# One-hot rows by transposes instead of DMA at the start of an attention and snake-MLP kernel, and the preparation of batch 0 dealt out anew

## The chip, the cores and the metric

The kernel runs on one core of one Trainium2 chip. The metric is the device time of one execution in microseconds (us). A time here is the median of several executions. Executions of one kernel mostly agree within 0.3 to 0.5%, but a few lie 0.3 to 0.7% higher. One core only is in use, so no two dies can be compared.

PE is the tensor engine (PEld its weight loads), DVE the vector engine, ACT the scalar engine, POOL the engine that here casts to bf16 and issues most loads, SP the engine that issues most other DMAs.

## The reference, cut to what matters

```python
q_assign = argmax(q_n @ c_n)          # nearest of 16 centroids, per token; k likewise
mask = q_assign[..., :, None] == k_assign[..., None, :]
attn = softmax(where(mask, q @ k.T / 8, -1e9))     # 4 batches, 8 heads, 768 tokens, 64 wide
x = (attn @ v) as 3072 x 512
h = x @ w_in;  out = (h + sin(alpha*h)**2 / alpha) @ w_out     # 512 -> 2048 -> 512
```

## The kernel before

The mask is folded into the score matmul. Each q and k column has 64 rows of data and 16 more rows that hold the one-hot of its centroid, so that one matmul over 80 rows gives scores and mask together. A *pair* is two heads; a batch has four pairs, and a pair takes 12 *steps*. One step is a score matmul (one k tile of 128 against 768 q), an exponential on ACT, and PV matmuls.

A pair must be prepared before its steps begin. Four *transpose units* (`prep_T`) turn q and k of both heads, each through one PSUM bank, which DVE or ACT then empties. A *routing unit* multiplies by the centroids, DVE finds the maximum and makes the one-hot (`prep_hot`), and DMAs carry it from its 128-partition layout to rows 64 to 79 of `QK` (`prep_move`, eight DMAs of one pair). A plan says at which step each of these stands.

```python
    def head_move(m, h, engs):                      # rows of one head, four DMAs
        for g in range(4):
            hf, t = divmod(g, 2)
            engs[t].dma_start(out=QK[D:D+NHC, m % NQK, h, t]..., in_=s["ohT"][32*g:32*g+NHC, :, 0:QS])
    # ... (cut) the start:
    warmup(2)
    head_asn(0, 0, M0)                               # routing matmuls, pair 0, head 0
    prep_cast(0, 0)
    for i in range(4):
        prep_hot(0, i, QS)                           # DVE: transpose, max, one-hot, transpose back
    prep_T(0, 2, SA[0][:, 0:512], "act")
    prep_T(0, 3, M1, "act")
    head_move(0, 0, [nc.sync, nc.scalar])
    load_qk(2)
    # ... (cut)
    head_move(0, 1, [nc.sync, nc.sync])
    prep_T(1, 0, M2, "act")                          # pair 1, all four, ahead of the first score
    prep_T(1, 2, M1)
    prep_T(1, 1, M0, "act")
    prep_T(1, 3, OB)
    load_v(1)
    warmup(1)
    # ... (cut) the plan of batch 0: (pair, transpose units at, routing unit at, casts at)
        (1, (), 1, (0, 0)),
        (2, ((0, 4), (2, 5), (1, 6), (3, 7)), 8, (7, 8)),
        # ...
    for m, i in {3: 5, 4: 10, 5: 12, 6: 18, 7: 22}.items():   # loads of q and k at
        at(i, lambda m=m: load_qk(m, eng=nc.gpsimd))
    at(39, alpha)                                    # one PE transpose, three small DVE operations
```

A PE transpose that must wait for its bank holds up the score matmul written after it: in the changed kernel below, the second score comes at 12.66 us, behind a transpose that waited until 12.28.

The softmax here doesn't subtract the row's maximum and nothing guards it: scores larger than these inputs give would overflow.

Of the kernel before, what the change touches and what calls it, by code (L numbers as in the profile page):

```python
# [10 lines left out]
BF16 = mybir.dt.bfloat16  # L11
# [4 lines left out]
P = 128  # L16
# [6 lines left out]
def kernel(  # L23
# [11 lines left out]
    nc = tc.nc  # L35

    B, H, S, D = q.shape
    NHC = centroids.shape[1]
# [6 lines left out]
    HS = S // 2  # L45
    QS = S // 4
# [22 lines left out]
    OB = psum.tile([P, 512], F32, name="OB")  # L69
    M0 = psum.tile([P, 512], F32, name="M0")  # L70
    M1 = psum.tile([P, 512], F32, name="M1")
    M2 = psum.tile([P, 512], F32, name="M2")

    ident_f = const.tile([P, P], F32, name="ident_f")
    ident_b = const.tile([P, P], BF16, name="ident_b")
# [6 lines left out]
    NQK = 6  # L82
    KR = D + NHC
    QK = const.tile([96, NQK, 2, 2, S], BF16, name="QK")
# [6 lines left out]
    st = [dict() for _ in range(NP)]  # L91
# [10 lines left out]
    def bank():  # L102
        while True:
            i = turn[0] % 3
            turn[0] += 1
            if i not in held:
                return banks[i]


    def load_qk(m, parts=1, eng=None):  # L110
        b, hp = pair_of[m]
        s = st[m]
        for nm in ("q32", "k32"):
            s[nm] = ldp.tile([P, 2, NJ * D], F32, tag=nm, name=nm)
        for i in range(parts):
            n = 2 // parts
            for nm, src in (("q32", q), ("k32", k)):
                (eng or nc.sync).dma_start(
                    out=s[nm][:, n * i : n * i + n, :],
                    in_=src[b, 2 * hp + n * i : 2 * hp + n * i + n].rearrange(  # L120
                        "h (p j) d -> p h (j d)", j=NJ
                    ),
                )
# [11 lines left out]
    def prep_T(m, g, bk=None, eng="dve"):  # L135

        s = st[m]
        if "T32" not in s:
            s["T32"] = trp.tile([P, 4, HS], F32, tag="T32", name="T32")
        h, t = divmod(g, 2)  # L140
        src = s["q32" if t == 0 else "k32"]
        bk = bank() if bk is None else bk
        for jj in range(NJ2):
            nc.tensor.transpose(  # L144
                out=bk[:, P * jj : P * jj + P],
                in_=src[:, h, P * jj : P * jj + P],
                identity=ident_f,
            )
        if eng == "dve":
            nc.vector.tensor_scalar_mul(  # L150
                out=s["T32"][:, g, :], in0=bk[:, 0:HS], scalar1=1.0 / QDIV
            )
        else:
            nc.scalar.activation(
                out=s["T32"][:, g, :], in_=bk[:, 0:HS], func=ACTF.Copy, scale=1.0 / QDIV
            )
# [24 lines left out]
    def prep_cast(m, h, eng=None):  # L181
        s = st[m]
        for par in range(2):
            src = s["T32"][D * par : D * par + D, 2 * h : 2 * h + 2, :]
            if m < NPE:
                nc.gpsimd.tensor_copy(  # L186
                    out=QK[0:D, m % NQK, h, :, HS * par : HS * par + HS], in_=src
                )
                continue
            for t in range(2):  # L190
                nc.gpsimd.tensor_scalar(  # L191
                    out=QK[0:D, m % NQK, h, t].rearrange("c (n i a) -> c i n a", i=4, a=32)[
                        :, 2 * par : 2 * par + 2
                    ],
                    in0=src[:, t].rearrange("c (i n a) -> c i n a", i=2, a=32),
                    scalar1=1.0 / QDIV,
                    scalar2=1.0,
                    op0=ALU.mult,
                    op1=ALU.mult,
                )  # L200

    def prep_v(m):
        nc.gpsimd.tensor_copy(out=VX[m % NVX][:, :, :, 0:D], in_=st[m]["v32"])  # L203
# [18 lines left out]
    def head_asn(m, h, bk):  # L222

        s = st[m]
        hp = pair_of[m][1]
        for g in range(4):
            hf, t = divmod(g, 2)
            nc.tensor.matmul(
                out=bk[32 * g : 32 * g + 32, 0:QS],
                lhsT=cnB[:, 2 * hp + h, :],  # L230
                rhs=s["T32"][:, 2 * h + t, QS * hf : QS * hf + QS],
                start=True,
                stop=True,
            )
        s["asn"] = bk[:, 0:QS]
# [69 lines left out]
    def head_move(m, h, engs):  # L305
        s = st[m]
        for g in range(4):
            hf, t = divmod(g, 2)
            engs[t].dma_start(
                out=QK[D : D + NHC, m % NQK, h, t].rearrange("c (par n) -> c par n", par=2)[  # L310
                    :, :, QS * hf : QS * hf + QS
                ],
                in_=s["ohT"][32 * g : 32 * g + NHC, :, 0:QS],
            )


    def area(i):
        return SA[(i // ASTEPS + i) % 2]

# [40 lines left out]
    def x_T(m, bk=None):  # L360
        b, hp = pair_of[m]
        xs = st[m]["xs"]
        xt_ps = (bank() if bk is None else bk).bitcast(BF16)[:, 0:S]
        for j in range(NJ):
            nc.tensor.transpose(
                out=xt_ps.rearrange("c (i j a) -> c j i a", i=4, j=NJ)[:, j],
                in_=xs[:, j, :, :],
                identity=ident_b,
            )
        nc.vector.tensor_copy(out=xT[:, hp, :], in_=xt_ps)  # L370
        st[m].clear()
# [127 lines left out]
    def warmup(n):  # L499
        for _ in range(n):  # L500
            nc.tensor.matmul(
                out=SA[1][:, 512:1024],
                lhsT=warm[:, 0:P],
                rhs=warm[:, P:640],
                start=True,
                stop=True,
            )
# [5 lines left out]
        out=csq, in0=c_sb, scalar=1.0, in1=c_sb, op0=ALU.mult, op1=ALU.mult, accum_out=cnrm  # L513
# [7 lines left out]
        out=cn_dup, in0=c_sb.unsqueeze(1).to_broadcast([P, 2, D]), scalar1=crn[:, 0:1]  # L521
# [4 lines left out]
    for h0, h1 in ((0, 1), (1, H)):  # L526
        for par in range(2):
            rows = slice(D * par, D * par + D)
            nc.vector.tensor_copy(
                out=cnB[rows, h0:h1, NHC * par : NHC * par + NHC],  # L530
                in_=OB[rows, NHC * h0 : NHC * h1].rearrange("p (h c) -> p h c", c=NHC),
            )
    etab = const.tile([P, 1], F32, name="etab")
    nc.scalar.activation(out=etab, in_=crn, func=ACTF.Exp)
    warmup(2)
    head_asn(0, 0, M0)
    prep_cast(0, 0)
    for i in range(4):
        prep_hot(0, i, QS)
    prep_T(0, 2, SA[0][:, 0:512], "act")  # L540
    prep_T(0, 3, M1, "act")
    head_move(0, 0, [nc.sync, nc.scalar])
    load_qk(2)
    prep_cast(0, 1)
    prep_v(0)
    head_asn(0, 1, OB)
    for i in range(4):
        prep_hot(0, i, QS)
    head_move(0, 1, [nc.sync, nc.sync])
    prep_T(1, 0, M2, "act")  # L550
    prep_T(1, 2, M1)
    prep_T(1, 1, M0, "act")
    prep_T(1, 3, OB)
    load_v(1)
    warmup(1)
    alpha_col = const.tile([P, NF], F32, name="alpha_col")
    ralpha = const.tile([P, NF], F32, name="ralpha")

# [3 lines left out]
    def at(i, fn):  # L562
        plan.setdefault(i, []).append(fn)
# [21 lines left out]
    def prep_new(m, k0):  # L585
# [4 lines left out]
        at(k0 + 17, lambda: prep_cast(m, 1))  # L590
        hot_steps(m, k0 + 8)

    for m, make, asn, cast in (
        (1, (), 1, (0, 0)),
        (2, ((0, 4), (2, 5), (1, 6), (3, 7)), 8, (7, 8)),
        (3, ((0, 12), (1, 14), (2, 16), (3, 17)), 20, (14, 18)),
        (4, ((0, 19), (1, 23), (2, 24), (3, 26)), 32, (24, 28)),
        (5, ((0, 28), (1, 30), (2, 31), (3, 34)), 38, (31, 35)),
        (6, ((0, 35), (1, 36), (2, 37), (3, 40)), None, (37, 41)),
    ):  # L600
        pair_steps(m, make, asn, cast)
    for g, i in enumerate((41, 42, 43)):
        at(i, lambda g=g: prep_T(NHP + 3, g))
    for h in range(2):
        at(ASTEPS + 4 + 2 * h, lambda h=h: prep_cast(NHP + 3, h))
    hot_steps(NHP + 3, ASTEPS + 7)
    for m, i in {3: 5, 4: 10, 5: 12, 6: 18, 7: 22}.items():
        at(i, lambda m=m: load_qk(m, eng=nc.gpsimd))
    late = []
    pacer = const.tile([1, 1], BF16, name="pacer")  # L610
    for b in range(1, B):
        for n in range(NHP):
            m = NHP * b + 3 + n
            if NPE <= m < NP:
                prep_new(m, ASTEPS * b + STEPS * n)
                if m < 3 * NHP:
                    late.append(m)
                else:
                    at(2 * ASTEPS - 1, lambda m=m: load_qk(m, eng=nc.gpsimd))
# [4 lines left out]
    for m in range(NP):  # L624
        if m % NHP != NHP - 1:
            if m < NHP:
                at((18, 29, 44)[m], lambda m=m: x_T(m))
            elif m % NHP == 2:
                at(STEPS * (m + 1) + 4, lambda m=m: x_T(m))
            else:  # L630
                at(STEPS * (m + 1) + 5, lambda m=m: x_D(m))
# [8 lines left out]
        nc.vector.tensor_scalar_add(out=ralpha, in0=alpha_col, scalar1=1e-9)  # L640
        nc.vector.reciprocal(out=ralpha, in_=ralpha)

    at(39, alpha)
    def load_w_in(n):
        nc.gpsimd.dma_start(
            out=w_in_bf[:, :, 512 * n : 512 * n + 512],
# [26 lines left out]
    for b in range(B):  # L673
        base = ASTEPS * b
        fill = Fill(b - 1) if b else None
        for r in range(ASTEPS):
            i = base + r
# [105 lines left out]
```

## Time and profile before

| | before |
|---|---|
| time, median | 313.26 us (312.94 to 313.51, 4 executions) |
| granted clock of the profiled execution | 1.000 |
| first score matmul | 11.39 us |
| first and last exponential of batch 0 start | 11.91 and 52.94 us |

So a wait on PE in the early stage is time lost, unless something else was to be waited for anyway.

The timeline of PE around the first score (start, length, engine, line, operation; in brackets the idle time before it and what ended it):

```profile
9.44 0.52 PE L144 MATMUL M<-ident_f,k 128*128 128x128 f32 x3 [0.21 <-DMA k<-in_k_dram]
9.79 0.49 PE L144 MATMUL OB<-ident_f,k 128*128 128x128 f32 x3
10.12 0.38 PE L501 MATMUL S<-gT 128*128 128x512 bf16 x1
11.39 0.38 PE L326 MATMUL S<-QK 80*128 80x512 bf16 x1 [0.89 <-DMA QK<-ohT]
11.61 0.27 PE L327 MATMUL S<-QK 80*128 80x256 bf16 x1
11.71 0.38 PE L326 MATMUL S<-QK 80*128 80x512 bf16 x1
```

The first score waits 0.89 us for the DMA of the one-hot rows, and the second follows 0.3 us later. That wait is what the change goes after. The largest waits of PE from 9 to 60 us (total, number, longest; that of L425, at 59.74 us, is already past batch 0):

```profile
PE S L326 <- DMA QK<-ohT: 1.2, 2, 0.9
PE S L425 <- DVE gT L450: 0.6, 1, 0.6
PE M L144 <- DVE T L150: 0.6, 1, 0.6
```

From the start times of the exponentials in the trace, a step takes 0.69 to 0.74 us with no unit in it, 0.85 to 0.87 us with a transpose unit, and 1.2 to 1.4 us around a routing unit.

### The profile page before, as it was taken

How to read it: one execution, taken by the hardware profiler on the slowest of the kernel's cores; microseconds unless marked ns; L12 is line 12 of the kernel's file. 1: busy time of each engine (PE TensorE's matmuls, PEld its weight loads, DVE VectorE, ACT ScalarE, POOL GpSimd, SP SyncE). 2: the span in 40 equal slices, each digit the busy share in tenths (PEclk: the TensorE clock that was granted, in tenths of full speed). 3: DMA queues.
4: the chain of work that ended last, by engine and by line, in shares of the span. 5: the costliest groups of instructions: out<-in, count | busy, mean ns of one | idle time of the engine just before them, and what ended most of it. 6: DMA issues, size and time to landing. Idle time of an engine off the chain costs nothing.

```text
span 312.8 us, 7228 instructions
## 1 busy us (share of the span) xinstructions
PE 302.7 (97%) x2750; PEld 179.9 (58%) x2750; DVE 208.9 (67%) x367; ACT 239.5 (77%) x324; POOL 139.0 (44%) x222
## 2 busy tenths in 40 slices
PE   8899998999999999999999999999999999999994
PEld 3466776455456656555556556555556666555443
DVE  4777796688866876677867877686935313687711
ACT  6589988787679998688679998688679999777200
POOL 5979997109506099985006079980001190000000
PEclk9999999999999999999999999999999999999999
DMA  7549996958753567991044477420011121000032
GB/s 232 146 159 292 310 232 128 196 93 285 233 135 79 106 163 171 261 347 60 0 124 113 98 171 163 114 84 2 0 67 49 37 49 39 34 0 2 0 134 69
DMA packets 28674, 38.92 MB, mean 124 GB/s; under 512 B 5072, under 2 KB 22496, under 8 KB 28640
## 3 DMA queue, kind: packets, MB, share of 16 engines
q0 software_dynamic: 10240, 21.11, 25.8%
q1 hardware_dynamic: 18160, 17.30, 20.6%
q8 instruction: 22, 0.36, 0.5%
q14 instruction: 12, 0.10, 0.1%
q10 hardware_dynamic: 240, 0.06, 0.1%
HBM read 27.30 MB, written 6.29 MB: 107 GB/s over the span
## 4 chain that ended last, share of the span: by engine, by line
PE 86%; DVE 5%; ACT 4%; DMA 2%; issue 1%; SPq 1%; ACTq 0%; DVEq 0%
PE M L394 19%; PE S L425 17%; PE S L326 12%; PE OB L341 10%; PE M L425 8%; PE S L327 6%; PE OB L394 5%; PE M L214 3%; DMA QK<-ohT 2%; PE S L394 2%; ACT pT L332 2%; PE M L144 2%; DVE gT L450 2%; ACT s_sb L438 1%; DVE T L150 1%; DVE u_sb L446 1%
## 5 line engine op out<-in xcount | busy, mean ns | idle before, releaser
L332 ACT ACTIVATE pT<-S 128x768 bf16<-128x768 f32 x192 | 143.7, 810 | 17.6 <-PE S L327 16.1
L394 PE MATMUL M<-w_out_bf,gT 128*128 128x512 bf16 (+1 forms) x288 | 90.7, 373 | 0.2
L326 PE MATMUL S<-QK 80*128 80x512 bf16 x192 | 72.9, 380 | 1.5 <-DMA QK<-ohT 1.2
L425 PEld LDWEIGHTS <-w_in_bf 128*128 128x128 bf16 x512 | 49.3, 98 | 37.9 <-issue 1.8
L341 PEld LDWEIGHTS <-pT 128*128 128x128 bf16 x1152 | 56.1, 97 | 21.4 <-issue 0.5
L425 PE MATMUL S<-xT,w_in_bf 128*128 128x512 bf16 x352 | 65.0, 326 | 0.7 <-DVE gT L450 0.6
L341 PE MATMUL OB<-VX,pT 128*128 128x65 bf16 x1152 | 61.3, 193 | 0.6 <-DVE xs L353 0.4
L438 ACT ACTIVATE s_sb<-S,alpha_col 128x768 bf16<-128x768 f32 (+2 forms) x45 | 39.3, 885 | 23.7 <-PE S L425 16.1
L394 PEld LDWEIGHTS <-gT 128*128 128x128 bf16 x400 | 39.0, 97 | 30.7 <-issue 5.4
L327 PE MATMUL S<-QK 80*128 80x256 bf16 x192 | 51.9, 270 | 0.0
L191 POOL TENSOR_SCALAR QK<-T 64x384 bf16<-64x384 f32 x64 | 34.9, 546 | 37.9 <-DMA T<-Tq 33.8
L450 DVE SCALAR_TENSOR_TENSOR gT<-u_sb,ralpha,S 128x768 bf16<-128x768 bf16 (+2 forms) x45 | 44.7, 996 | 9.7 <-ACT u_sb L443 6.8
L387 POOL DMA_DIRECT2D xT<-xq x48 | 25.8, 544 | 29.0 <-DVE xq L379 28.0
L186 POOL CAST QK<-T 64x768 bf16<-64x768 f32 x32 | 27.1, 848 | 7.7 <-DVE T L150 3.5
L425 PE MATMUL M<-xT,w_in_bf 128*128 128x512 bf16 (+1 forms) x160 | 29.9, 326 | 0.0
L352 DVE RECIPROCAL rec<-OB 128x6 f32<-128x6 f32 x32 | 6.2, 193 | 34.8 <-PE OB L341 34.8
L446 DVE TENSOR_TENSOR u_sb<-s_sb 128x768 bf16<-128x768 bf16 (+2 forms) x41 | 23.7, 580 | 7.0 <-ACT s_sb L438 7.0
L327 PEld LDWEIGHTS <-QK 80*128 80x128 bf16 x192 | 18.8, 98 | 16.1 <-issue 2.0
L203 POOL CAST VX<-v 128x768 bf16<-128x768 f32 x16 | 13.7, 859 | 28.7 <-issue 27.8
L438 ACT ACTIVATE s_sb<-M,alpha_col 128x512 bf16<-128x512 f32 (+1 forms) x40 | 20.9, 573 | 7.2 <-PE M L425 7.2
L450 DVE SCALAR_TENSOR_TENSOR gT<-u_sb,ralpha,M 128x512 bf16<-128x512 bf16 (+1 forms) x40 | 22.8, 611 | 5.4 <-ACT u_sb L443 5.0
L394 PE MATMUL OB<-w_out_bf,gT 128*128 128x512 bf16 (+1 forms) x80 | 26.2, 358 | 0.1
(83 smaller groups left out, 282.2 us busy)
## 6 DMA issues: line engine op xcount, KB each, us to landing
T<-Tq SPq DMA_DIRECT2D x64, 96.0 KB, 2.5
out_dram<-o_sb SPq DMA_DIRECT2D x23, 256.0 KB, 2.1
v<-in_v_dram POOLq DMA_DIRECT2D x14, 384.0 KB, 4.6
q<-in_q_dram POOLq DMA_DIRECT2D x13, 384.0 KB, 6.4
k<-in_k_dram POOLq DMA_DIRECT2D x13, 384.0 KB, 6.8
w_in_bf<-in_moe_w_in_dram POOLq DMA_DIRECT2D x4, 512.0 KB, 7.9
w_out_bf<-in_moe_w_out_dram POOLq DMA_DIRECT2D x4, 512.0 KB, 9.1
xT<-xq POOLq DMA_DIRECT2D x48, 24.0 KB, 2.2
```

Of the source, the lines that this page charges most:

```text
L186: nc.gpsimd.tensor_copy(out=QK[0:D, m % NQK, h, :, HS * par : HS * par + HS], in_=src)
L191: nc.gpsimd.tensor_scalar(out=QK[0:D, m % NQK, h, t].rearrange("c (n i a) -> c i n a", i=4, a=32)[:, 2 * par : 2 * par + 2], in0=src[:, t] ...
L326: nc.tensor.matmul(out=dst[:, 0:512], lhsT=lhsT, rhs=T[:, 0, 0:512], start=True, stop=True)
L327: nc.tensor.matmul(out=dst[:, 512:S], lhsT=lhsT, rhs=T[:, 0, 512:S], start=True, stop=True)
L332: nc.scalar.activation(out=pT, in_=area(i)[:, 0:S], func=ACTF.Exp, scale=escale)
L341: nc.tensor.matmul(out=o3[:, j, :], lhsT=pT[:, P * j : P * j + P], rhs=VX[m % NVX][:, h, jof(m // NHP, kt), :], start=(kt == 0 and j == 0) ...
L387: nc.gpsimd.dma_start(out=xT[32 * g : 32 * g + 32, 0:2, QS * i : QS * i + QS], in_=xq[0].rearrange("p (h g n) -> p h g n", h=2, g=4)[32 * ...
L394: nc.tensor.matmul(out=bk[:, lo:hi], lhsT=gT[:, f, P * mt : P * mt + P], rhs=w_out_bf[:, f, lo:hi], start=(f == 0), stop=(f == NF - 1),)
L425: nc.tensor.matmul(out=ar[lo // 512][:, 0 : hi - lo] if isinstance(ar, tuple) else ar[:, lo:hi], lhsT=lhsT, rhs=xT[:, kk, :].rearrange("c ...
L438: nc.scalar.activation(out=s_sb[:, lo:hi], in_=src, func=ACTF.Sin, scale=alpha_col[:, f : f + 1])
L446: nc.vector.tensor_tensor(out=u_sb[:, lo:hi], in0=s_sb[:, lo:hi], in1=s_sb[:, lo:hi], op=ALU.mult)
L450: nc.vector.scalar_tensor_tensor(out=gT[:, f, lo:hi], in0=u_sb[:, lo:hi], scalar=ralpha[:, f : f + 1], in1=src, op0=ALU.mult, op1=ALU.add,)
```

## The change

Its intent: the first head's rows need not go through DVE and DMA. PE transposes the one-hot, and ACT and DVE copy 16 partitions of PSUM straight into `QK`, so the scores can begin sooner. To gain more, the transpose units of pair 1 are taken out of the start and put into steps 0, 1 and 5, and pair 1 is routed one head at a time (steps 4 and 8). The units, loads and the alpha step of the other pairs are shifted to match. Cut to its core:

```diff
+    def head_rows(m, h, bks):
+        ...  # 12 transposes of oh[:, par, i, 0:16] into two banks, then five copies:
+        put(0, 0, both, 0, n, "act")
+        put(1, 0, 0, 0, 4, "dve")
+        put(0, 1, both, 0, n, "dve")
+        put(1, 0, 0, 4, n, "act")
+        put(1, 0, 1, 0, n, "act")
+        rows_late[0] = lambda: put(1, 1, both, 0, n, "dve")
 ...
-    warmup(2)
+    warmup(1)
 ...
-    for i in range(4):
+    for i in range(3):
         prep_hot(0, i, QS)
 ...
-    head_move(0, 0, [nc.sync, nc.scalar])
     load_qk(2)
+    head_rows(0, 0, (M2, M0))
 ...
-    head_move(0, 1, [nc.sync, nc.sync])
-    prep_T(1, 0, M2, "act")
-    prep_T(1, 2, M1)
-    prep_T(1, 1, M0, "act")
-    prep_T(1, 3, OB)
+    head_move(0, 1, [nc.sync, nc.gpsimd])
+    rows_late[0]()
+    prep_T(1, 0, M1)
     load_v(1)
-    warmup(1)
 ...
+    for g, i in ((1, 0), (2, 1), (3, 5)):
+        at(i, lambda g=g: prep_T(1, g))              # the first of these takes bank M1 again
+    for h, a in ((0, 4), (1, 8)):
+        ...  # head_asn, prep_hot, prep_cast at a; the rest of prep_hot and head_move on SP at a + 1
-        (1, (), 1, (0, 0)),
-        (2, ((0, 4), (2, 5), (1, 6), (3, 7)), 8, (7, 8)),
+        (2, ((0, 6), (2, 7), (1, 10), (3, 11)), 14, (10, 12)),
 ...                                                 # pairs 3 to 6 shifted by up to 4 steps
-    for m, i in {3: 5, 4: 10, 5: 12, 6: 18, 7: 22}.items():
+    for m, i in {4: 11, 5: 13, 6: 18, 7: 22}.items():
 ...                                                 # load of pair 3 at step 7, held back by a "pacer"
-    at(39, alpha)
+    at(12, alpha)
```

## The prediction

> **What bounds the kernel now.** Busy shares: PE 97%, ACT 77%, DVE 67%. The change touches only the start and batch 0's attention: from the first instruction to the last softmax exponential, about 53.8 us. The first score matmul starts at 11.39 us (timeline) after 0.89 us of idle PE ("DMA QK<-ohT"). From the first exponential (11.91) to the end of the 48th (about 53.7) are 41.8 us, 0.87 us a step. An exponential alone repeats every 0.70 to 0.73 us; many steps are PE-bound: the chain of waits shows 0.22+0.11+0.18 us of scores and PV per step, plus 0.36 per transpose unit, 0.34 for an x transpose, 0.78 for a routing matmul unit of a pair. Steps take 0.87 with a unit, 0.71 without, 1.2 to 1.4 with a routing unit. [...] pair 1's rows took 4.78 us in flight beside loads, and step 12 waited 0.3 us.
>
> **What the change does.**
> 1. Pair 0, head 0: two DVE transposes (0.64 us) and four DMAs (issue from 8.41, landing near 11.3) go. Twelve small transposes (estimate 0.7 in all, from 0.34 per six x transposes) and five PSUM copies (estimate 0.2 to 0.5 each) come. The one-hot is ready at 7.7, or 7.5 with one warm-up matmul fewer. First score near 9.2 to 9.5 instead of 11.4: about 2 us earlier.
> 2. But the next scores stand in the PE queue behind the transpose of pair 1's head 0 k, which takes bank M1, the same as the q transpose just before it. That bank is emptied by DVE only after head 1's hot chain (2.0 us in this trace) and the late copy, at about 11.6. So the second score matmul comes near 12, the second exponential near 12.5 against 12.6 before: this wait eats most of the 2 us.
> 3. Three transpose units move from the start into steps 0, 1, 5 (3 x 0.36 PE), and two half routing units (0.53 each) replace one of 0.78. That is 1.3 us more PE work; four steps without a unit are filled (0.2 us slack each). Net +0.5 us.
> 4. Pair 1 head by head: four moves instead of eight before step 12, but begun at step 4 instead of step 1. Chain: matmul 0.55, one-hot 2.4, four issues of 0.6, landing 2 to 3: 7.5 to 8 us, against 7.2 to step 12. A wait of 0 to 1 us.
> 5. Alpha (about 1 us of DVE) leaves step 39 for 12; steps 40 to 47, where PE waited on DVE's backlog (intervals 0.96, 1.63, 1.17), should give 0.5 to 1 us back.
>
> Later code is the same and should shift as a block.
>
> **Prediction.** First exponential 2 us earlier, last 0 to 1.5. Time 312.7 us, 311.3 to 314.1 eight times in ten. Faster by over 2%: 0.02; within 2%: 0.97; slower by over 2%: 0.01.
>
> **What would show it.** First score at 9 to 9.6; a PE wait of about 2 us "until DVE T" between first and second score; exponential 12 within 0.7 us of 22.2; no interval of 1.6 near step 44; stretches after batch 0 as long as before.
>
> **What would make it wrong.** DVE ordering the evacuation of M1 earlier (then 1.5 to 2 us better); the rows of pair 1's head 0 landing late beside loads (1 to 2 us worse); PSUM copies of 16 partitions slower than estimated; DVE falling behind in the first 12 steps.

The estimates for copies and landings can be set beside the trace of before: copies out of PSUM take 0.17 to 0.28 us (64 partitions, 16 or 112 columns, DVE) and 0.49 us (128x384, ACT), and the first four row moves landed 1.8 to 2.2 us after their issue, two of pair 1's, beside loads, after 5.3 and 5.7 us.

## More of the kernel before

"Granted clock" is the share of full TensorE clock that the profile records, 1.000 at best.

The head of the profile's page: span, busy shares, and two rows of the 40 slices (a digit is a tenth).

```profile
span 312.8 us, 7228 instructions
...
PE   8899998999999999999999999999999999999994
...
PEclk9999999999999999999999999999999999999999
```

PE is busy almost throughout, and its clock is at full speed in every slice, from 5.61 us on at least: the record of the clock begins only there.

## The result, and the profile after

| | before | after |
|---|---|---|
| time, median | 313.26 us | 317.57 us (317.25 to 318.38, 4 executions) |
| granted clock of its executions | 1.000 (the profiled one) | 0.993, 0.989, 0.995, 0.995 |
| first score matmul | 11.39 us | 9.21 us |
| first and last exponential of batch 0 | 11.91, 52.94 | 9.73, 57.22 |

The ratio is 1.0142 (95% interval 1.0119 to 1.0165). A ratio is the mean time of one kernel's runs over that of the other's of the same rounds, so it is not quite the ratio of the medians quoted. Executions over 1.5% slower than the fastest of the same kernel are left out of the means. The change makes the kernel 4.3 us slower, and that is clear of the noise, although it is under 2%.

Where batch 0's exponentials start (us, from the traces) shows at which steps the time was lost:

| exponential | 0 | 1 | 5 | 8 | 12 | 24 | 27 | 39 | 47 | 191 (the last) |
|---|---|---|---|---|---|---|---|---|---|---|
| before | 11.91 | 12.62 | 15.76 | 18.35 | 22.16 | 32.13 | 34.45 | 45.15 | 52.94 | 263.28 |
| after | 9.73 | 13.18 | 17.83 | 20.49 | 25.49 | 36.68 | 39.98 | 50.68 | 57.22 | 267.57 |
| difference | -2.18 | +0.56 | +2.07 | +2.14 | +3.33 | +4.55 | +5.53 | +5.53 | +4.28 | +4.29 |

Everything is decided by exponential 47. From there to the last one both kernels take 210.3 us. Five pieces are to be explained: 2.7 us from 0 to 1, 1.5 from 1 to 5, 1.2 from 8 to 12, 2.2 from 12 to 27, and 1.25 given back from 39 to 47.

The same rows of the page as before:

```profile
span 315.6 us, 7264 instructions
...
PE   7698899999999999999999999999999999999995
...
PEclk9989999999999999999999999999999999999999
```

PE's first slices are less full, and in the third slice (15.8 to 23.7 us) the granted clock is no longer full. The span differs by less than the times do, because the last store took longer to land in the profiled execution of before (3.04 us against 1.69); that execution took 314.59 us, more than any of the four in the table. PE at the same place as before:

```profile
8.69 0.55 PE L144 MATMUL M<-ident_f,q 128*128 128x128 f32 x3
9.21 0.38 PE L358 MATMUL S<-QK 80*128 80x512 bf16 x1
9.43 0.27 PE L359 MATMUL S<-QK 80*128 80x256 bf16 x1
12.28 0.55 PE L144 MATMUL M<-ident_f,k 128*128 128x128 f32 x3 [2.58 <-DVE T L150]
12.66 0.38 PE L358 MATMUL S<-QK 80*128 80x512 bf16 x1
...
14.37 0.84 PE L373 MATMUL OB<-VX,pT 128*128 128x65 bf16 x12
15.02 0.62 PE L358 MATMUL S<-QK 80*128 80x512 bf16 x1
15.43 0.42 PE L359 MATMUL S<-QK 80*128 80x256 bf16 x1
...
16.91 0.61 PE L358 MATMUL S<-QK 80*128 80x512 bf16 x1
```

The first score comes 2.2 us earlier, as intended. Then PE sits idle for 2.58 us before the k transpose of pair 1, and the second score cannot pass it. Some two microseconds after that wait the same matmul takes 0.62 us that took 0.38 us before. That is not more work: it is a slower clock. DVE's timeline shows what bank M1 waited for:

```profile
9.14 0.38 DVE L243 STREAM_TRANSPOSE asT<-OB 128x192 f32<-128x192 f32 x1
9.56 0.35 DVE L246 TENSOR_REDUCE amax<-asT 128x12 f32<-128x192 f32 x1
10.02 0.56 DVE L263 TENSOR_TENSOR oh<-asT,amax 128x192 bf16<-128x192 f32 x1
10.61 0.64 DVE L283 STREAM_TRANSPOSE ohT<-oh 128x192 bf16<-128x192 bf16 x2
11.28 0.35 DVE L339 COPY QK<-M 16x384 bf16<-16x384 bf16 x1
11.67 0.56 DVE L150 TENSOR_SCALAR T<-M 128x384 f32<-128x384 f32 x1
```

The last line empties M1. It stands behind the whole one-hot chain of head 1 and the late copy. ACT was idle from the end of the first exponential (10.54) to 13.19.

The trace also records the granted clock by itself, and it changes only at whole multiples of 3.41 us (in the changed kernel full for 10.24 us, half for 3.41, full for 296.96). Cut at these boundaries (placed to about 0.1 us), PE's busy time looks so (stretch, its length, busy time and count of matmuls, granted clock, DMA share, GB/s):

```profile
7.56:10.97 3.41, 2.12 (x25) 1.00 0.91 326
10.97:14.38 3.41, 1.86 (x13) 1.00 0.20 33
14.38:17.80 3.42, 3.42 (x37) 0.50 0.29 104
17.80:21.21 3.41, 3.41 (x42) 1.00 0.00 1
```

One stretch in which PE was busy for only 1.86 us is followed by one at exactly half clock. The waits of PE for the same stretch after the change, small ones cut:

```profile
PE M L144 <- DVE T L150: 2.6, 1, 2.6
PE S L358 <- DMA QK<-ohT: 1.9, 2, 1.1
...
PE S L358 <- issue: 0.4, 1, 0.4
```

The wait of 1.1 us is at step 12, for the rows of pair 1's first head. One of 0.78 us is at step 27, for pair 2's rows, and the 0.40 us at step 24 are at the first use of pair 2. For the last the profile names no releaser, but the row that step 24 needs, issued at 31.66 us, took 4.4 us and landed at 36.02, and the score starts at 36.11. The chain of waits shows how long these small DMAs were under way (start, length):

```profile
20.56 0.59 SPq L309
21.15 0.04 issue
21.20 3.47 DMA QK<-ohT
...
31.66 0.59 SPq L295
32.25 0.04 issue
32.29 7.05 DMA QK<-ohT
```

### The profile page after: what moved, and what is told of

It is laid out like the page before. It is cut to its first block, busy times and chain, and to the rows that moved or that the text cites. A ratio compares the mean times of both kernels' runs of the same rounds, so it can differ in the third digit from the quotient of the medians.

```text
span 315.6 us, 7264 instructions
## 1 busy us (share of the span) xinstructions
PE 303.4 (96%) x2768; PEld 180.5 (57%) x2768; DVE 210.1 (67%) x376; ACT 240.2 (76%) x325; POOL 140.5 (45%) x225
## 4 chain that ended last, share of the span: by engine, by line
PE 83%; DVE 7%; DMA 4%; ACT 3%; issue 1%; SPq 1%; DVEq 0%; ACTq 0%
PE M L426 18%; PE S L457 16%; PE S L358 12%; PE OB L373 10%; PE M L457 7%; PE S L359 6%; PE OB L426 5%; DMA QK<-ohT 3%; PE M L214 3%; PE S L426 2%; DVE gT L482 2%; ACT s_sb L470 1%; PE M L144 1%; DVE u_sb L478 1%; DMA c_sb<-in_centroids_dram 1%
## 5 line engine op out<-in xcount | busy, mean ns | idle before, releaser
L373 PE MATMUL OB<-VX,pT 128*128 128x65 bf16 x1152 | 62.0, 194 | 0.7 <-DVE xs L385 0.4
```

The costliest lines, as they stand in the source:

```text
L373: nc.tensor.matmul(out=o3[:, j, :], lhsT=pT[:, P * j : P * j + P], rhs=VX[m % NVX][:, h, jof(m // NHP, kt), :], start=(kt == 0 and j == 0) ...
```

## The experiments

The theory: PE stands idle for bank M1, which brings on a window at half clock; two later waits for DMA rows do the rest. The main rival: the extra and re-dealt work costs the time, and the clock is incidental. Twelve kernels were run, four to a chip; all gave the right result. E1 to E4 shared a chip on which before spread widely (312.16 to 314.86, median 314.61 us). For E5 to E8 before's median was 312.92, for E9 to E12 313.13.

| run | kernel | median us | before there | ratio (95% interval) | granted clocks |
|---|---|---|---|---|---|
| E1 | after, ACT empties M1 | 314.37 | 314.61 | 1.0022 (0.9977 to 1.0067) | 1.000, 0.994, 1.000, 1.000 |
| E2 | after, wait filled with dummy matmuls | 316.35 | 314.61 | 1.0077 (1.0030 to 1.0124) | 1.000 four times |
| E3 | after, later loads | 317.56 | 314.61 | 1.0106 (1.0051 to 1.0160) | 0.989, 0.995, 0.989, 0.989 |
| E4 | after, pair 1's rows from two queues | 316.23 of the three fast (316.81 of all four) | 314.61 | 1.0086 (1.0031 to 1.0141) | 0.994, 0.994, 0.987 (without the 628 us execution) |
| E5 | before plus rows by transposes alone | 314.83 | 312.92 | 1.0057 (1.0036 to 1.0077) | 0.999 to 1.000 |
| E6 | before plus dealing alone | 317.58 | 312.92 | 1.0143 (1.0114 to 1.0171) | 0.989 to 0.995 |
| E7 | after, three waits removed | 313.12 | 312.92 | 1.0013 (0.9982 to 1.0044) | 0.998 to 1.000, once 0.995 |
| E8 | before, alpha at step 12 | 312.72 | 312.92 | 1.0000 (0.9970 to 1.0030) | 0.998 to 1.000, once 0.995 |
| E9 | before plus a long stall | 317.01 | 313.13 | 1.0122 (1.0098 to 1.0146) | 0.995 four times |
| E10 | before plus a short stall | 315.79 | 313.13 | 1.0078 (1.0048 to 1.0107) | 0.995, 1.000, 0.995, 0.995 |
| E11 | before, alpha at step 22 | 312.10 | 313.13 | 0.9966 (0.9947 to 0.9986) | 0.999 to 1.000 |
| E12 | dealing alone, later loads | 313.32 | 313.13 | 1.0004 (0.9985 to 1.0023) | 0.998 to 1.000 |

Start times of exponentials in the profiled executions. The start itself shifts between executions of the same code: exponential 0 stands between 11.55 (E10) and 12.32 us (E11) in those with the start of before, and between 9.73 and 10.90 in those with the changed start. In E3 (10.90) a load of q landed late; in E2 (10.24) the recorded clock begins at 7.50 us, in the changed kernel at 4.14. So differences along a row count for more than a single figure.

| exponential | 0 | 1 | 5 | 8 | 12 | 24 | 27 | 39 | 47 |
|---|---|---|---|---|---|---|---|---|---|
| E1 | 9.93 | 10.97 | 14.24 | 16.82 | 21.49 | 33.29 | 36.29 | 46.99 | 53.53 |
| E2 | 10.24 | 13.94 | 17.16 | 19.75 | 24.69 | 35.81 | 38.59 | 49.29 | 55.84 |
| E3 | 10.90 | 14.03 | 19.19 | 21.80 | 26.78 | 37.43 | 39.83 | 51.05 | 57.62 |
| E5 | 12.22 | 12.93 | 16.66 | 19.25 | 22.96 | 32.93 | 35.56 | 46.27 | 53.92 |
| E6 | 12.09 | 12.80 | 15.77 | 18.19 | 21.69 | 35.21 | 38.77 | 49.68 | 56.22 |
| E7 | 9.86 | 10.89 | 14.20 | 18.60 | 22.03 | 32.67 | 35.38 | 46.21 | 53.04 |
| E8 | 11.94 | 12.65 | 15.80 | 18.38 | 22.57 | 32.89 | 35.20 | 45.91 | 52.47 |
| E11 | 12.32 | 13.03 | 16.17 | 18.76 | 22.47 | 32.46 | 34.78 | 45.49 | 52.03 |
| E12 | 12.07 | 12.78 | 15.75 | 18.17 | 21.67 | 32.42 | 34.82 | 45.81 | 52.67 |

### E1: take the wait away

```diff
-    prep_T(1, 0, M1)
+    prep_T(1, 0, M1, "act")
```

> Pair 1's first q transpose leaves bank M1 by the scalar engine (idle then) instead of the vector engine's queue; all else as in the changed kernel. Theory (an idle wait of PE for bank M1, and a half clock that follows it): the wait of 2.6 us between first and second score goes, the granted clock is 1.000, the second exponential starts near 10.5 to 11 us instead of 13.2, the last one 3.5 to 4.5 us earlier than in the changed kernel, time 313.2 to 314.2 us. Rival (more routing and transpose work dealt into the steps is what costs): at most 1 us gained, time 316.5 or more.

Measured: the second exponential starts at 10.97 us, the clock is 1.000 in three of four executions, and the last exponential is at 53.53 instead of 57.22 us. One word in the program gives 3.7 us back (3.2 by the medians, which come from different chips). The theory holds and the rival fails here; the median, 314.37 us, is 0.2 over the expected range, on a chip on which before was slower too. The single execution at 0.994 took 315.28 us against 314.27 to 314.41 for the other three. What remains against before is +0.59 us at exponential 47, although the first one is 2 us earlier. The waits at steps 12 to 27 are still there: from 12 to 27 this kernel takes 14.8 us, before 12.3.

### E2: keep the wait, fill it with work

```diff
+    at(0, lambda: warmup(11))        # 11 dense dummy matmuls after the first score
     for g, i in ((1, 0), (2, 1), (3, 5)):
```

> The changed kernel with 11 dense dummy matmuls (about 2.4 us) after the first score, inside the wait for bank M1: the wait for the vector engine stays, PE is not idle in it. Theory (the idle PE brings on the half clock): granted clock 1.000, scores of 0.38 us throughout, second exponential still near 13.2 us, the sixth 1.5 to 1.7 us earlier, time 315.7 to 316.3 us. Rival (the slow clock has another cause): clock still near 0.994, time 317.3 or more.

The PE timeline of this run at the same place:

```profile
9.94 0.27 PE L359 MATMUL S<-QK 80*128 80x256 bf16 x1
10.26 2.32 PE L533 MATMUL S<-gT 128*128 128x512 bf16 x10
13.03 0.55 PE L144 MATMUL M<-ident_f,k 128*128 128x128 f32 x3 [0.45 <-DVE T L150]
...
15.51 0.38 PE L358 MATMUL S<-QK 80*128 80x512 bf16 x1
```

The transpose still waits for DVE until 13.03 us, but PE was doing useless matmuls. The scores stay at 0.38 us, and the clock is 1.000 in all four executions. From exponential 1 to 5 it takes 3.22 us, as before (3.14), where the changed kernel took 4.65. So in this stretch idleness brought the slow clock on, not the delay as such and not the re-dealt work; it cost 1.4 us. The median, 316.35 us, is just above what was expected.

### E3: loads moved away from pair 2's rows

```diff
-    for m, i in {4: 11, 5: 13, 6: 18, 7: 22}.items():
+    for m, i in {4: 11, 5: 19, 6: 22, 7: 26}.items():
-        (15, load_w_in, 0),
+        (21, load_w_in, 0),
```

> The changed kernel with the loads of pairs 5, 6, 7 and the first slice of w_in postponed (steps 19, 22, 26, 21 instead of 13, 18, 22, 15), so that pair 2's one-hot rows do not fly beside them. Theory (the 0.8 us wait of step 27 is rows delayed by loads [...]): that wait goes, the fourth row move lands within 3.5 us of its issue instead of 7, time 0.6 to 1.2 us under the changed kernel, 316.4 to 317.0. Rival (rows are late because the routing was begun at step 14 rather than 8, loads or not): wait stays above 0.5 us, time 317.3 or more.

Inconclusive in time. Exponentials 24 to 27 take 2.40 us instead of 3.30, so the wait at step 27 is gone, as the theory has it. But exponentials 27 to 39 take 0.5 us longer. About 0.2 of it is pair 6's load, now too late (q and k land at 47.05 and 47.92 us, their transposes start at 47.09 and 48.05); 0.3 lies at step 27, and I did not find its cause. The profile also shows a wait of 1.06 us for a q load, but at 9.99 us, ahead of the first score, where nothing was changed. And in three of four executions the granted clock was 0.989: two windows at half clock instead of one. In the profiled execution the first of them follows a window in which PE was busy for only 1.02 us, since the wait for the q load and most of that for M1 (1.59 us here) fell together. The median did not move.

### E4: pair 1's first rows from two queues

```diff
-head_move(1, h, [nc.sync] * 2)
+head_move(1, h, [nc.sync, nc.sync if h else nc.gpsimd])
```

> The changed kernel with the k rows of pair 1's first head issued from the Pool queue and the q rows from SP, instead of all four from SP. Theory (step 12 waits 1.1 us because four issues of 0.6 us stand in one queue after a routing begun at step 4): rows land about 1.2 us sooner, wait at step 12 under 0.3 us, time 0.7 to 1.2 us under the changed kernel, 316.4 to 316.9. Rival (the landing, delayed by pair 3's load, decides): wait stays at 0.8 us or more, time 317.3 or more.

The profiled execution fell on the 628 us outlier, with matmuls near half speed from end to end (a score matmul of 512 columns took 0.67 us in the mean, 0.38 in the changed kernel), so its step 12 cannot be read. Of the three others, two with a clock of 0.994 took 316.13 and 316.23 us, where the changed kernel took 317.25 to 317.72 at 0.993 to 0.995, though on another chip; the third took 317.40 us at 0.987 (the changed kernel 318.38 at 0.989). That is 1.0 to 1.6 us under the changed kernel, about the expected size, but the cause is not shown by it. E7 has the same edit with a usable profile, among two others.

### E5: the rows by transposes alone, in before

The start of before, with `head_rows` in place of `head_move(0, 0)` and of the one-hot's transposes; pair 1's four transpose units stay where they were.

```diff
-    for i in range(4):
+    for i in range(3):
         prep_hot(0, i, QS)
 ...
-    head_move(0, 0, [nc.sync, nc.scalar])
     load_qk(2)
+    head_rows(0, 0, (M2, M0))        # all five copies and the late one at once
```

> The kernel before with one part of the change alone: pair 0's first head's rows by transposes and PSUM copies; the four transposes of pair 1 stay ahead of the first score, the dealing is that of before. Theory: no PE wait above 1.5 us, clock 1.000, first exponential near 10.9 us instead of 11.9, but the routing unit of step 1 waits for the vector engine as before, so the third exponential comes only 0.1 to 0.5 us earlier; time 0 to 0.6 us under before. Rival (the transposes and copies themselves are dear): time above before.

This expectation was wrong: it is 0.57% slower than before, and the first exponential is no earlier (12.22 us). The rows' transposes hold banks M2 and M0, which pair 1's transposes want next; PE waits 0.60 us for ACT's copy out of M2, and the first score comes at 11.69 us. So replacing the DMA brings nothing by itself. It seems to pay only if pair 1's transposes leave the start, which is the reason for the re-dealing. Of this kernel's loss 0.6 us lies between exponentials 1 and 2 (1.43 against 0.83) and about 0.75 us after batch 0; I followed neither.

### E6: the dealing alone, in before

Before's start and its whole-pair routing of pair 1 at step 1; the plan of pairs 2 to 6, loads, pacer, x transposes and alpha as in the changed kernel.

```diff
         (1, (), 1, (0, 0)),
-        (2, ((0, 4), (2, 5), (1, 6), (3, 7)), 8, (7, 8)),
+        (2, ((0, 6), (2, 7), (1, 10), (3, 11)), 14, (10, 12)),
 ...     # and so on for pairs 3 to 6; loads at 7, 11, 13, 18, 22; alpha at 12
```

> The kernel before with the other part alone: units, loads and alpha dealt out as in the changed kernel; start and pair 1's whole-pair routing at step 1 as before. Theory: no half clock; waits for pair 2's rows at steps 24 to 27 (0.7 to 1.5 us together), exponentials 12 to 27 take 1.5 to 2.5 us longer than before, 39 to 47 take 1 to 1.3 us less; net time within 1 us of before (0 to +1). Rival (dealing accounts for most of the 4.3 us): 2.5 us or more over before.

By its time the rival wins: 317.58 us, as slow as the whole change, although the wait for M1 cannot occur. PE's timeline at step 24, and PE's busy time by the clock's own boundaries:

```profile
31.48 0.53 PE L144 MATMUL M<-ident_f,k 128*128 128x128 f32 x3
34.31 0.59 PE L326 MATMUL S<-QK 80*128 80x512 bf16 x1 [2.30 <-POOL QK L186]
```

```profile
30.60:34.01 3.41, 1.41 (x20) 1.00 0.90 133
34.01:37.43 3.42, 3.12 (x24) 0.50 1.11 329
```

It is the same sequence, a wait of PE and then half clock, at another place. My expectation had "no half clock" and was wrong there. A wait of 2.30 us at step 24 leaves the window 1.41 us busy, and the next has half the clock. The rows were issued from 26.8 us on, beside loads of q, k and w_in, and took 6.2 us (median) to land. The profile names a cast on POOL as releaser, but that cast ended at 33.73 us. The k row that step 24 needs, issued at 27.96, took 6.3 us and landed at 34.22, just before the score. So the change holds two separate faults, each of which alone is about enough for the loss. In the full change the second one shows as smaller waits (0.40 and 0.78 us): its pair 2 begins later, so that less was left to wait for.

### E7: all three waits taken away

The edits of E1 and E4, and loads of pairs 4 to 7 at 9, 18, 20, 24 and of the first slice of w_in at 21.

> The changed kernel with all three waits taken away: scalar engine evacuates bank M1, pair 1's first rows go from two queues, loads of pair 4 at step 9, of pairs 5, 6, 7 and w_in at 18, 20, 24, 21. Theory: clock 1.000, step 12 waits under 0.3 us, steps 24 to 27 under 0.4 together; last exponential of batch 0 near 51.5 us (53.5 with the first of the three alone, 52.95 before); time 1 to 2 us under before. Rival (the waits hide one another, or the extra work fills the room): time within 0.5 us of before.

The waits at steps 12 and 24 to 27 are gone from the list of PE's waits: 8 to 12 takes 3.43 us (after: 5.00) and 24 to 27 takes 2.71 (after: 3.30). That agrees with E4's edit, but does not isolate it (see step 4 below). The time is 313.12 us, 4.5 us under the changed kernel, but no better than before, and the last exponential is at 53.04, not near 51.5: the rival of this run is right. Of the 2.0 us gained at the start, 0.5 is gone by step 5. Another 0.5 us is lost after batch 0 (exponentials 47 to 191 take 210.8 us here and 210.9 in E1, against 210.3), which I did not follow. The profiled execution, with 313.83 us the slowest but one, then waits 1.67 us at step 6 for the rows of pair 0's second head, one of which took 3.98 us to land. From 12 to 27 it takes 1.06 us more than before, with no wait in it. That agrees with the work moved there: before has eight transpose units, one routing unit and an x transpose at these steps, and after has one routing unit (0.78 us on PE) and alpha (0.16) more.

### E8 and E11: alpha alone

```diff
-    at(39, alpha)
+    at(12, alpha)        # E8;   at(22, alpha) in E11
```

> The kernel before with alpha's transpose and its three vector operations at step 12 instead of 39, nothing else. Theory (what the changed kernel gives back over steps 39 to 47, 1.26 us, is the vector engine freed of alpha): exponentials 39 to 47 take 6.5 to 6.9 us instead of 7.8, step 12 at most 0.2 us longer, time 0.7 to 1.2 us under before. Rival (it comes from the units dealt differently): under 0.3 us gained.

E8: exponentials 39 to 47 take 6.56 us instead of 7.79, as in the changed kernel (6.54). So the part given back, 1.25 us, is DVE freed of alpha's three small operations (0.16, 0.60 and 0.25 us in before). But 11 to 15 takes 0.65 us longer (3.92 against 3.27), and the ratio to before is 1.0000. Of the 0.65 us, 0.38 is a longer wait for pair 1's rows at step 12 (0.67 us, before 0.29). E10, where alpha stayed at 39, has that wait too (0.74), so it is not shown to come from alpha; the other 0.27 us stand at the step with alpha in it. The mechanism held, the gain did not.

> The kernel before with alpha at step 22, a step without a unit, instead of 39. Theory (alpha at 12 gave back 1.23 us over steps 39 to 47 and lost 0.7 of it around step 12): exponentials 39 to 47 take 6.5 to 6.7 us instead of 7.8, 21 to 27 at most 0.3 us longer, time 0.5 to 1 us under before, under both kernels. Rival (the vector engine pays elsewhere whatever the step): within 0.2 us of before.

E11: 39 to 47 takes 6.54 us, 21 to 27 takes 4.66 (before 4.64), and the time is 312.10 us, a ratio of 0.9966 with an interval clear of 1 (before spread from 312.26 to 315.46 us on this chip, E11 from 311.83 to 312.51). This is a version faster than both kernels. It is one number in the plan of before.

### E9 and E10: idleness alone, in before

Nothing of the change. At step 25 DVE does a memset and four (E10: two) transposes of a scratch tile, and one PE transpose waits for them.

```diff
+    def stall():
+        nc.vector.memset(gT[:, 14, 0:HS], 0.0)
+        for _ in range(4):                       # E10: range(2)
+            nc.vector.transpose(out=gT[:, 15, 0:HS], in_=gT[:, 14, 0:HS])
+        nc.tensor.transpose(out=bank().bitcast(BF16)[:, 0:P], in_=gT[:, 15, 0:P], identity=ident_b)
+    at(25, stall)
```

> The kernel before with nothing of the change, but with a memset and four vector transposes at step 25 that one PE transpose waits for: PE idle 2.3 to 3 us once. Theory (windows of 3.41 us; [...]): in most executions one window at half clock follows, granted clock near 0.995, time 3.5 to 5 us over before. Rival (an idle wait costs only its own length): clock 1.000, 2 to 3 us over before.

> The same with two vector transposes: PE idle 1.1 to 1.8 us once. Theory: [...] no half clock in most executions, granted clock 1.000, time 1 to 2 us over before. Rival (any wait beyond a microsecond brings the slow window on): clock 0.995, 3 us or more over before.

My estimate came from the windows known then: those of 1.02 (E3), 1.41 (E6) and 1.86 us (the changed kernel) of PE busy time were followed by half clock, one of 2.12 us (the changed kernel) was not. So the long stall was to bring half clock on, and the short one not.

PE's busy time by the clock's boundaries, first E9, then E10:

```profile
33.90:37.32 3.42, 1.30 (x14) 1.00 1.02 357
37.32:40.73 3.41, 3.41 (x34) 0.50 1.01 236
```

```profile
32.41:35.83 3.42, 1.66 (x18) 1.00 1.06 326
35.83:39.24 3.41, 3.41 (x30) 0.50 1.04 317
```

E9: PE idle for 2.99 us, clock 0.995 in all four executions, +3.9 us. E10: PE idle for 1.76 us, and here my expectation was wrong: three of four executions had the half clock too. The stall was near the upper end of what I had allowed for, and it fell whole into one window. So in the profiled execution (0.995) 1.76 us of idleness was enough. The one execution of E10 at full clock took 314.95 us, the others 315.79 to 316.16: the slow window cost 0.8 to 1.2 us on top of the wait.

### E12: the dealing alone, with the loads moved away

E6 with the loads of E7.

> The kernel with the dealing alone, with the loads of pairs 4 to 7 and of w_in at steps 9, 18, 20, 24, 21 instead of 11, 13, 18, 22, 15, so that pair 2's rows fly free. Theory (dealing alone lost 2.3 us at step 24 to rows landing late beside loads, and a half clock after it): wait at step 24 under 0.4 us, rows land within 3.5 us of issue, clock 1.000, time 3 to 4.5 us under the dealing alone, 312.8 to 314.3. Rival (casts on Pool, named by the profile, hold step 24): wait above 1.5 us, time above 316.

Measured 313.32 us, 4.3 us under E6; no PE wait at step 24 (24 to 27 takes 2.40 us, E6 3.56), and the clock 0.998 to 1.000 in all six executions. Of the rows issued between 26 and 31 us, E6's view of DMA issues comes first, E12's second (size, median us to landing):

```profile
QK<-ohT SPq DMA_DIRECT2D x6, 12.0 KB, 6.2
```

```profile
QK<-ohT SPq DMA_DIRECT2D x7, 12.0 KB, 2.1
```

The rows held step 24, and the loads beside them made them late. (POOL issues the loads too, so its casts also move in E12; that they were not the cause rests on the landing time in E6.)

## Why the prediction was wrong, point by point

- **First score 2 us earlier** (step 1): right. 9.21 us was measured, 9.2 to 9.5 predicted. There is some luck in the figure: over the profiled executions of the two starts, exponential 0 moves by 1.9 us in the mean (10.13 against 12.00).
- **The wait for bank M1** (step 2): the place, the cause and the direction were right. Predicted: the second exponential near 12.5 against 12.6, so that the wait "eats most of the 2 us". Measured: 13.18 us, a wait of 2.58 us, 0.56 us behind before. This term was 0.6 to 0.7 us too small.
- **The step that failed** is the same step 2, in treating the wait as costing only its length. Here the idle PE (1.86 us busy in 10.97 to 14.38 us) is followed by a window of 3.41 us at half clock (0.50, 14.38 to 17.80). It costs 1.5 us between exponentials 1 and 5 (E2: 1.4 us of it undone by filling the wait). My text does not mention the clock, although the kernel's warm-up matmuls, one of which the change removes from just before the first score, should have made me ask.
- **Work moved into the steps, "net +0.5 us"** (step 3): about right for what it counts, pair 1's units. With the waits removed (E7), 0 to 5 takes 0.47 us more than before. What it left out is pair 2's routing unit, moved from step 8 to 14, and what alpha costs at step 12: in E7, 8 to 12 takes 0.38 us less than before and 12 to 27 takes 1.06 us more.
- **Pair 1's rows, "a wait of 0 to 1 us"** (step 4): 1.09 us was measured, just outside. The row waited for was issued 1.28 us after the first of the four, in one queue, and then took 3.47 us beside pair 3's load. In E7, with two queues, the same row is issued 0.62 us after the first and takes 1.95 us, because pair 3's load starts after it; PE's wait at step 6 also gave it time. So one queue and the load both stand in the way, and their shares are not separated.
- **Not foreseen at all:** pair 2's rows. I weighed pair 1's routing against its deadline and not pair 2's, which the change moved from step 8 to 14, among the loads. Its waits are 0.40 and 0.78 us in the full change, and 2.30 us plus a half clock in E6. The 0.40 us, too, are a late row: it landed 0.09 us before the score.
- **The give-back by alpha** (step 5): right. 1.25 us was measured against 0.5 to 1 predicted, and E8 and E11 show its cause.
- **Later stretches unchanged**: right, 210.3 us in both.

The sum of the miss: I had put the last exponential of batch 0 at 0 to 1.5 us earlier, and it is 4.28 us later. Taking the middle, that is 5.0 us. Of these the longer wait is 0.65, the half clock 1.5, step 12 about 0.6 (1.09 less the 0.5 allowed), and the stretch from 12 to 27 about 1.7 (2.2 less the 0.5 allowed), less about 0.5 for alpha. That makes 4.0; the other microsecond is spread over small differences that I have not assigned.

What stays open: how busy a window must be. In batch 0, windows of 1.02 to 1.86 us of PE busy time were followed by half clock; the least busy ones that were not had 2.12 us (the changed kernel, from 7.56) and 2.19 us (E11, from 8.81). But this is no border: at the very end of E9, E10 and E11 windows of 1.69, 1.83 and 1.64 us were followed by a window that the trace records at full clock (no matmul ran in it). Nor is it shown that the granted clock goes by PE's busy time; that is only what the profile offers to set beside it. Why E3 mostly had two slow windows is also open: its first slow window was 3.16 us busy at half speed, and yet the next was slow too.

## What to carry to other kernels

Waits of PE of 1.76 to 2.99 us were followed by half clock here (E10, E6, the changed kernel and E9, in their profiled executions), and the half clock cost 0.8 to 1.5 us on top of the wait (E10, E2 against the changed kernel). So cost such a wait as its length plus about 1 us, an estimate from these runs, and find it in the bank a transpose reuses and in the queue of the engine that empties that bank: here one word, which sent an evacuation to the idle engine, gave back 3.7 us. When units are dealt out anew, check each pair's last DMA against the step that needs it and against the loads in flight beside it, because a 12 KB transfer took 2.1 us with little beside it (median, E12) and 6.2 us beside loads (median, E6; up to 7.05 in the changed kernel). When a start-up gain of 2 us has to be bought with more work in the stage that follows, look for slack on the limiting engine's neighbours first; moving alpha's three small DVE operations to an empty step gained 1 us where the change lost 4.3.
